# Attention decode with a gated MLP on one core: the order of PE's work behind the turned projection

## The chip, the core and the metric

One core of a Trainium2 chip runs the whole program in one launch. The metric is device time in microseconds; the median of the shown runs counts. Engines: PE (TensorE, matmuls), DVE (VectorE), ACT (ScalarE), POOL (GpSimd), SP (SyncE, which issues the transfers).

## The reference, cut to what matters

```
x = A_x                                    # 4 x 1 x 512
sa, ca, ga, sb, cb, gb = split(silu(c) @ w_mod)
h = layernorm(x) * (1 + ca) + sa
x = x + ga * attention(h)                  # A: 32 heads, 4096 cached keys, 128 per head, 4 batch rows
h = layernorm(x) * (1 + cb) + sb
x = x + gb * mlp(h)                        # B: gelu(h @ w_in), halves z1 and z2,
                                           #    z1 * (w_sp * layernorm(z2) + b_sp) @ w_out
# attention: q = h @ wq; p = softmax(q . k / sqrt(128)); (p @ v) @ wo
```

One query per batch row meets 4096 cached keys and values in each of 32 heads, all in bf16: 268 MB of cache are read once. The MLP is small (512 to 1792, and 896 to 512).

## The kernel before, in words

The cache is worked through in tiles of four heads (NT = 32 of them, numbered by i). The first 30 come in pairs, eight heads of one batch row; the last two, N0 = 30 and L = 31, hold the last eight heads of the last batch row (BL = 3), four each, and are not paired. For each tile DVE multiplies keys by the query (mult, L384) and sums over the head's width together with PE (reduce_d, L392; sum8, L415; sum_rest, L404), DVE finds the maximum, and ACT makes the exponentials (exps, L458), which it writes to pbd. Then PE forms the products with the value tile.

These products come in two forms. pv and pv_some (L513) take four positions of the cache at once: the stationary operand is a slice of pbd (16 columns for an unpaired tile), 512 columns of values stream through, and four such matmuls are placed side by side in the array, at columns 0, 32, 64 and 96. What they leave in PSUM (the tile ops, one of two) holds wanted blocks and others. o_pick takes the wanted ones out on DVE (one L522 and three L526, into osb), and o_cols (L538) adds up and turns them into columns with a matmul; o_scale (L561) divides by the softmax sum and writes to oTp. The second form, o_last with part 2, 3 or 4 (L549), takes a position at a time with the values stationary and gives columns at once, in the PSUM tile qps. For the last tile L, parts 0 and 1 (32 of 128 positions each) go the first way, and parts 2, 3 and 4 (32, 16 and 16) the second; o_first (L555) adds the picked result of parts 0 and 1 to the same sum in qps. The parts follow the five pieces in which the last value tile is loaded (TAIL, load, L142).

The projection with wo: for all heads but the last four, a head's columns have to be dealt out first to fit the layout in which wo was loaded (deal, L640, PE; dealt, L652 and L658, DVE; then o_proj4, L617). The last four heads need none (o_proj, L607). For three head groups the projection makes rows (project, L670); turn (L682, L617 and L607) turns these and adds the heads of the other three batch rows: the turned projection. x1 and the statistics of its layer norm follow for all batch rows (normed: L234, L219, L224, L240, L243, L219, L224, L228, L229). The last batch row lacks its last eight heads there. They are added as `last` afterwards (L801 to L804), and this row gets statistics of its own (L805, a third L219). Then come the MLP (gates L852, L877), the gate weights (L885) and the output (L922, L923).

normed sends two matmuls to PE with DVE work between them, and takes two hooks, which the call before does not use: `then` runs after the first matmul is put in the queue, `last` before the second.

The order of the work is written out by hand: each engine runs its instructions in the order in which the code calls them, and waits only where data or a buffer is not ready. All transfers of this part are issued from SP in order: value tile N0 (4 MB into buffer C), the five pieces of value tile L (into buffer B), two halves of w_in, w_out, two pieces of the MLP's last weights. Eight semaphores go around among the transfers, so that an issue waits for the landing of the eighth transfer before it: w_out's for value tile N0, the next one's for the first piece of tile L, the output's for the third piece.

Of the kernel before, what the change touches and what calls it, by code (L numbers as in the profile page):

```python
# [49 lines left out]
def kernel(  # L50
# [25 lines left out]
    NJ = SK * HQ // P  # L76
    NP = 2 * NJ
    R = P // HQ
    G = 4
    NT = B * H // HQ  # L80
    GP = H // HP - 1
    N0 = NT - 2
# [6 lines left out]
    L = NT - 1  # L89
# [18 lines left out]
    def ps_sm(shape, dtype=F32):  # L108
        return psum.tile(shape, dtype, name="sm", bufs=3)
# [98 lines left out]
    def bc(ap, n):  # L208
        return ap[:, None, :].to_broadcast([P, n, ap.shape[-1]])
# [7 lines left out]
    def across(rhs, mat):  # L217
        ps = ps_sm(list(rhs.shape))
        nc.tensor.matmul(ps, lhsT=mat, rhs=rhs, start=True, stop=True)  # L219
        return ps  # L220

    def summed(pool, ps, name):
        r = pool.tile([P, ps.shape[1]], F32, name=name)
        nc.vector.tensor_reduce(out=r, in_=ps, axis=AX.X, op=ALU.add)  # L224
        return r

    def rsqrt(dst, src, scale, bias=0.0):
        nc.scalar.activation(out=dst, in_=src, func=AF.Ln, bias=bias, scale=scale)  # L228
        nc.scalar.activation(out=dst, in_=dst, func=AF.Exp, scale=-0.5)  # L229

    def normed(pool, src, name, then=None, last=None):

        sb = pool.tile([P, B, DJ], F32, name=f"sb_{name}")
        nc.vector.tensor_copy(out=sb, in_=src.rearrange("p j b -> p b j"))  # L234
        m = across(sb, inv_d)
        if then:
            then()
        m = summed(pool, m, f"m_{name}")
        xc = pool.tile([P, DJ, B], F32, name=f"xc_{name}")
        nc.vector.tensor_tensor(out=xc, in0=src, in1=bc(m, DJ), op=ALU.subtract)  # L240
        sq = pool.tile([P, B, DJ], F32, name=f"sq_{name}")
        xb = xc.rearrange("p j b -> p b j")
        nc.vector.tensor_tensor(out=sq, in0=xb, in1=xb, op=ALU.mult)  # L243
        if last:
            last()
        v = summed(pool, across(sq, inv_d), f"v_{name}")
        rs = pool.tile([P, B], F32, name=f"rs_{name}")
        rsqrt(rs, v, 1.0, eps)
        return xc, rs
# [125 lines left out]
    def pair(i):  # L375
        return i < N0
# [124 lines left out]
    def ops_of(i):  # L501
        return opss[i // 2 % 2 if pair(i) else i % 2]

    def pv(i):
        n = (NP if pair(i) else NJ) // G
        pv_some(i, 0, n, n)

    def pv_some(i, m0, m1, end):
        pb, vt, rows = (pbd8, bufC, G * HP) if pair(i) else (pbds[:, i % 4], vts[i], G * HQ)
        for m in range(m0, m1):  # L510
            n = slice(m * G, (m + 1) * G)
            g = R * (m % 4)
            nc.tensor.matmul(  # L513
                ops_of(i)[g:g + rows], lhsT=pb[:, n, :], rhs=vt[:, n, :],
                start=(m < 4), stop=(m >= end - 4), tile_position=(0, g),
            )

    def o_pick(i):
        ops = ops_of(i)
        sel = sels[HP if pair(i) else HQ]  # L520
        osb = wk.tile([P, DH], F32, name="osb", bufs=2)
        nc.vector.tensor_scalar(  # L522
            out=osb, in0=ops[:, 0, :], scalar1=sel[:, 0:1], scalar2=None, op0=ALU.mult
        )
        for g in range(1, G):
            nc.vector.scalar_tensor_tensor(  # L526
                out=osb, in0=ops[:, g, :], scalar=sel[:, g:g + 1], in1=osb,
                op0=ALU.mult, op1=ALU.add,
            )
        st[i, "osb"] = osb  # L530

    def o_cols(i):
        if pair(i):
            op = ps_sm([P, P])
            nc.tensor.transpose(op, st.pop((i, "osb")), ident_f)
        else:
            op = ps_sm([P, HQ])
            nc.tensor.matmul(op, lhsT=st.pop((i, "osb")), rhs=sel4, start=True, stop=True)  # L538
        st[i, "op"] = op

    def o_last(i, part):
        n0, n1 = sum(TAIL[:part]), sum(TAIL[:part + 1])
        if part < 2:
            pv_some(i, n0 // G, n1 // G, sum(TAIL[:2]) // G)
            return
        if part == 2:
            st[i, "op"] = psum.tile([P, HQ], F32, name="qps", bufs=1)
        for k in range(n0, n1):
            nc.tensor.matmul(  # L549
                st[i, "op"], lhsT=vts[i][:, k, :], rhs=pbds[:, i % 4, k, :],  # L550
                start=(part == 2 and k == n0), stop=(k == NJ - 1),
            )

    def o_first(i):
        nc.tensor.matmul(st[i, "op"], lhsT=st.pop((i, "osb")), rhs=sel4, start=False, stop=False)  # L555

    def o_scale(i):
        op = st.pop((i, "op"))
        if not pair(i):
            q0 = (i - N0) * HQ  # L560
            nc.vector.tensor_tensor(  # L561
                out=oTp[:, NT // 2 - 1, q0:q0 + HQ], in0=op, in1=st.pop((i, "rz")), op=ALU.mult
            )
            return
        g, b = divmod(i // 2, B)
        if b == 0:
            st["P", g, "o"] = wk.tile([P, B, HP], F32, name="oU")
        o = st["P", g, "o"]
        nc.vector.tensor_reduce(
            out=o[:, b, :], in_=op.rearrange("p (c q) -> p q c", q=HP), axis=AX.X, op=ALU.add  # L570
        )
        if whole(i):
            nc.vector.tensor_tensor(
                out=oTp[:, g * B:g * B + b + 1], in0=o[:, 0:b + 1],
                in1=st.pop((i, "rz")).rearrange("p (b q) -> p b q", q=HP), op=ALU.mult,
            )
# [7 lines left out]
    tl = Arena(bufC, 32 * KB, 64 * KB)  # L584
# [28 lines left out]
    def o_proj4(wp, j, bs, start):  # L613

        od = st["od", GP, bs.start]
        for r in range(HQ):
            nc.tensor.matmul(  # L617
                wp[:, j, 0:bs.stop - bs.start], lhsT=wo_sb[:, GP * HP + r, j:D:DJ], rhs=od[:, r, :],
                start=start and r == 0, stop=False, skip_group_check=True,
            )  # L620
# [15 lines left out]
    def deal(k, bs=slice(0, B)):  # L636
        n, nb = HP if k < GP else HQ, bs.stop - bs.start
        pp = ps_sm([P, n, nb, n])
        for r in range(n):
            nc.tensor.matmul(  # L640
                pp[:, r], lhsT=picks[n][:, r, :],
                rhs=oTp[:, k * B + bs.start:k * B + bs.stop, 0:n], start=True, stop=True,
            )
        st["pp", k, bs.start] = pp
# [3 lines left out]
    def dealt(k, b0=0):  # L648
        pp = st.pop(("pp", k, b0))
        n, nb = pp.shape[1], pp.shape[2]  # L650
        ow = own if n == HP else own[:, 0:n * nb, 0:n]
        nc.vector.tensor_tensor(  # L652
            out=ow, in0=pp.rearrange("p r b h -> p (r b) h"),
            in1=bc(mask8 if n == HP else mask4, n * nb), op=ALU.mult,
        )
        od = late.tile([P, n, nb], BF16, name=f"od{k}{b0}")
        with nc.allow_low_precision("all but one term of each sum are zero"):
            nc.vector.tensor_reduce(  # L658
                out=od.rearrange("p r b -> p (r b)"), in_=ow, axis=AX.X, op=ALU.add
            )  # L660
        st["od", k, b0] = od
# [115 lines left out]
    nc.vector.tensor_tensor(out=acc, in0=wp, in1=gaT, op=ALU.mult)  # L777
    x1 = x1w[:, :, 0:B]
    nc.vector.tensor_tensor(out=x1, in0=acc, in1=xT, op=ALU.add)
    xc, rs2 = normed(tl, x1, "ln2")  # L780
    pv(N0)
    o_last(L, 0)
    o_pick(N0)
    o_cols(N0)
    o_scale(N0)
    o_last(L, 1)
    deal(GP, slice(BL, B))
    dealt(GP, BL)
    o_pick(L)
    o_last(L, 2)  # L790
    o_first(L)
    wp = ps_sm([P, DJ, 1])
    for j in range(DJ):
        o_proj4(wp, j, slice(BL, B), j == 0)
    o_last(L, 3)
    o_last(L, 4)
    o_scale(L)
    for j in range(DJ):
# [155 lines left out]
```

## Time and profile before

| | |
|---|---|
| runs shown | 665.11, 665.56, 667.5 us; median 665.56 |
| profiled execution | 667.08 us, span 665.04 us, mean granted clock of PE 0.744 |
| busy share of the span | PE 48%, DVE 86%, ACT 26%, POOL 3% |
| read from HBM | 282.73 MB, 425 GB/s over the span |
| L513 on tile N0 (32 matmuls) | from 643.73 us, for 3.59 us |
| L219, two norm matmuls | 641.90 and 643.20 us, 0.61 us each |
| pick on DVE (L522 and three L526) | from 647.38 and from 650.45 us |
| L549, 32 and 32 matmuls | from 649.98 and from 652.98 us |
| last o_scale (L561) | 654.01 us |
| issue of the output (L923) | 662.72 us |

Times inside the execution are microseconds from the start of its span. A line such as L513 is the line of the kernel before. The chain of waits goes back from the last instruction, at each step to what released it. Matmuls overlap in PE's pipeline, so their ends are modelled. The clock that PE was granted is given as a share of the full one.

### The profile page before, as it was taken

What the parts mean: (1) busy time and instruction counts of PE and PEld (TensorE: products, weight loads), DVE (VectorE), ACT (ScalarE), POOL (GpSimd) and SP (SyncE); (2) the same over time, 40 slices, a digit from 0 to 9 for tenths busy, and PEclk for the clock granted to TensorE, in tenths of its full rate; (3) what the DMA queues carried; (4) which work ended last, traced back from release to release, by engine and by line L of the source; (5) the groups of instructions that cost most, each with busy time, mean ns of one, the idle gap of its engine ahead of it and who ended that gap; (6) DMA issues with size and microseconds to landing.
All of it is one profiled execution on the core that took longest, in us unless ns stands there. A gap on an engine that the chain in (4) does not pass through costs nothing.

```text
span 665.0 us, 5225 instructions
## 1 busy us (share of the span) xinstructions
PE 318.1 (48%) x2134; PEld 137.4 (21%) x2134; DVE 571.1 (86%) x403; ACT 171.3 (26%) x284; POOL 20.0 (3%) x57
## 2 busy tenths in 40 slices
PE   1563543646152364625246461434646243465885
PEld 0221111212021121202112120211212021122344
DVE  3259999989898998989899897989989898999823
ACT  1210606032050604205060410506032050605212
POOL 3000000000000000000000000000000000003100
PEclk9988787857677786767778676787867578787865
DMA  8999999999999999999999999999999999999995
GB/s 362 451 431 430 441 435 442 435 442 435 434 410 441 435 430 441 435 438 439 422 434 442 422 427 441 438 438 442 422 434 435 430 434 439 416 437 430 425 411 205
DMA packets 9356, 283.07 MB, mean 426 GB/s; under 512 B 876, under 2 KB 2804, under 8 KB 3956
## 3 DMA queue, kind: packets, MB, share of 16 engines
q1 hardware_dynamic: 9312, 282.73, 98.6%
q8 instruction: 16, 0.26, 0.1%
q14 instruction: 8, 0.07, 0.0%
q10 hardware_dynamic: 20, 0.01, 0.0%
HBM read 282.73 MB, written 0.00 MB: 425 GB/s over the span
## 4 chain that ended last, share of the span: by engine, by line
DMA 60%; DVE 17%; PE 17%; ACT 4%; issue 1%; POOL 0%; SPq 0%; DVEq 0%; ACTq 0%
DMA bC<-in_A_v_cache_dram 44%; DMA bA<-in_A_k_cache_dram 12%; PE ops L513 10%; DVE bA L384 7%; DVE S L404 5%; ACT pbd L458 3%; PE red L392 3%; DMA bC<-in_w_mod_dram 3%; DVE bB L384 1%; DVE S L415 1%; DMA bC<-in_B_b_sp_dram 1%; PE sm L670 1%; PE qps L319 1%; DVE osb L526 1%; PE sm L311 1%
## 5 line engine op out<-in xcount | busy, mean ns | idle before, releaser
L458 ACT ACTIVATE pbd<-S,nb 32x256 bf16<-32x256 f32 x120 | 154.2, 1519 | 424.9 <-DVE nb L445 423.7
L384 DVE TENSOR_TENSOR bA<-bA,qbp 128x8192 bf16<-128x8192 bf16 x32 | 141.1, 4411 | 25.3 <-DMA bA<-in_A_k_cache_dram 25.3
L392 PE MATMUL red<-bB,ident_bf 128*128 128x512 bf16 x344 | 97.2, 442 | 116.4 <-DVE bB L384 116.3
L392 PE MATMUL red<-bA,ident_bf 128*128 128x512 bf16 x332 | 94.0, 443 | 113.6 <-DVE bA L384 113.4
L392 PEld LDWEIGHTS <-ident_bf 128*128 128x128 bf16 x676 | 73.2, 110 | 344.2 <-issue 176.2
L384 DVE TENSOR_TENSOR bB<-bB,qbp 128x8192 bf16<-128x8192 bf16 x28 | 123.7, 4417 | 15.0 <-DMA bB<-in_A_k_cache_dram 15.0
L513 PE MATMUL ops<-bC,pbd 128*32 128x512 bf16 (+1 forms) x992 | 88.4, 534 | 70.3 <-DMA bC<-in_A_v_cache_dram 65.3
L404 DVE TENSOR_REDUCE S<-bA 128x48 f32<-128x6144 bf16 x15 | 98.1, 6541 | 0.0
L404 DVE TENSOR_REDUCE S<-bB 128x48 f32<-128x6144 bf16 x14 | 91.6, 6542 | 0.0
L513 PEld LDWEIGHTS <-pbd 128*32 128x32 bf16 (+1 forms) x1008 | 37.4, 128 | 119.9 <-issue 65.1
L458 ACT ACTIVATION_READ_ACCUMULATOR pbd<-S,nb 32x1 f32 x120 | 58.6, 489 | 0.0
L415 DVE TENSOR_REDUCE S<-red 128x64 f32<-128x512 f32 x64 | 43.7, 683 | 4.3 <-PE red L392 4.3
L472 POOL TENSOR_TENSOR rsb<-maskd,rs 128x8 f32<-128x8 f32 x15 | 3.9, 260 | 581.3 <-ACT pbd L458 581.3
L384 DVE TENSOR_TENSOR bB<-bB,qbo 128x8192 bf16<-128x8192 bf16 x4 | 17.6, 4412 | 0.0
L526 DVE SCALAR_TENSOR_TENSOR osb<-ops,m,osb 128x128 f32<-128x128 f32 x45 | 15.8, 351 | 1.6
L491 PE MATMUL sm<-rsb,inv_d 128*128 128x32 f32 (+2 forms) x12 | 3.1, 356 | 15.2 <-POOL rsb L472 14.4
L458 ACT ACTIVATE pbd<-S,nM 32x128 bf16<-32x128 f32 x8 | 4.6, 576 | 13.7 <-POOL pbd L718 12.5
L283 DVE SCALAR_TENSOR_TENSOR bC<-sm,bC 128x16 f32<-128x16 f32 x1 | 0.2, 173 | 8.5 <-PE sm L269 8.5
L428 DVE TENSOR_REDUCE mrow<-S 128x1 f32<-128x256 f32 (+1 forms) x17 | 6.9, 404 | 0.6
L631 POOL COPY bA<-ident_bf 128x1024 bf16<-128x1024 bf16 (+1 forms) x2 | 6.5, 3272 | 0.0
L319 PE MATMUL qps<-bC 128*128 128x256 bf16 (+1 forms) x16 | 4.5, 383 | 4.1 <-ACT qbp L329 2.8
L360 DVE COPY modT<-sm 128x48 f32<-128x48 f32 x1 | 0.2, 208 | 7.0 <-PE sm L357 7.0
(160 smaller groups left out, 139.5 us busy)
## 6 DMA issues: line engine op xcount, KB each, us to landing
bA<-in_A_k_cache_dram SPq DMA_DIRECT2D x2, 4096.0 KB, 32.1
bC<-in_A_wq_dram SPq DMA_DIRECT2D x1, 4096.0 KB, 12.2
bB<-in_A_k_cache_dram SPq DMA_DIRECT2D x1, 4096.0 KB, 41.5
bB<-in_A_k_cache_dram SPq DMA_DIRECT2D x2, 2048.0 KB, 40.8
bC<-in_A_v_cache_dram SPq DMA_DIRECT2D x1, 4096.0 KB
bA<-in_A_wo_dram SPq DMA_DIRECT2D x3, 1024.0 KB, 36.8
bB<-in_A_v_cache_dram SPq DMA_DIRECT2D x3, 1024.0 KB, 17.4
bC<-in_w_mod_dram SPq DMA_DIRECT2D x1, 2560.0 KB, 17.9
```

Source lines behind the costliest of these rows:

```text
L311: nc.tensor.matmul(qr[R * q:R * (q + 1)], lhsT=hT[:, k, :], rhs=wq_v[:, k, gs, q, :], start=(k == 0), stop=(k == DJ - 1), tile_position=(0 ...
L319: nc.tensor.matmul(qp[:, 0:npair], lhsT=eb2[k][:, b].rearrange("p k q r -> p (k q r)"), rhs=qrow[:, h, k:2 * npair:2], start=(k == 0), sto ...
L384: nc.vector.tensor_tensor(out=kt, in0=kt, in1=bc(q, KC), op=ALU.mult)
L392: nc.tensor.matmul(red, lhsT=ident_bf, rhs=kt[:, :, m * rd:(m + 1) * rd], start=(m == 0), stop=(m == DH // rd - 1),)
L404: nc.vector.tensor_reduce(out=st[i, "S"][:, n0:NJ], in_=kts[i][:, n0:NJ, :], axis=AX.X, op=ALU.add)
L415: nc.vector.tensor_reduce(out=st[i, "S"][:, kc * KC:kc * KC + on_pe(i, kc)], in_=st.pop((i, "red", kc)), axis=AX.X, op=ALU.add,)
L428: nc.vector.tensor_reduce(out=mrow, in_=S, axis=AX.X, op=ALU.max)
L458: nc.scalar.activation(out=pbd8[r, :, 2 * q + h] if pair(i) else pbds[r, i % 4, :, q], in_=S[r, :], func=AF.Exp, bias=nM[r, h:h + 1], scal ...
L513: nc.tensor.matmul(ops_of(i)[g:g + rows], lhsT=pb[:, n, :], rhs=vt[:, n, :], start=(m < 4), stop=(m >= end - 4), tile_position=(0, g),)
L526: nc.vector.scalar_tensor_tensor(out=osb, in0=ops[:, g, :], scalar=sel[:, g:g + 1], in1=osb, op0=ALU.mult, op1=ALU.add,)
L631: nc.gpsimd.tensor_copy(out=picks[n].rearrange("p r (a u) -> p r a u", a=n), in_=ident_bf.rearrange("p (u r) -> p r u", r=n)[:, :, None, : ...
L670: nc.tensor.matmul(wp, lhsT=od[:, r, :], rhs=wo_sb[:, k * HP + r, :], start=(k == 0 and r == 0), stop=(k == GP - 1 and r == HP - 1),)
```

## The change

Only the calls behind the turned projection are put in another order; no operation is added or removed. The 32 products of tile N0 are divided into 8, 16 and 8: eight ahead of normed, sixteen in its hook `then` (after the first norm matmul), eight in its hook `last` (before the second). Part 1 of the last tile moves ahead of o_pick(N0), so that it stands right behind part 0. Part 2 stands ahead of o_pick(L). The projection of the last row's dealt heads (o_proj4) and part 3 now stand ahead of o_first, which adds the picked half.

```
-    xc, rs2 = normed(tl, x1, "ln2")
-    pv(N0)
+    nv = NJ // G
+    pv_some(N0, 0, nv // 4, nv)
+    xc, rs2 = normed(
+        tl, x1, "ln2",
+        lambda: pv_some(N0, nv // 4, 3 * nv // 4, nv), lambda: pv_some(N0, 3 * nv // 4, nv, nv),
+    )
     o_last(L, 0)
     o_pick(N0)
+    o_last(L, 1)
     o_cols(N0)
     o_scale(N0)
-    o_last(L, 1)
     deal(GP, slice(BL, B))
     dealt(GP, BL)
+    o_last(L, 2)
     o_pick(L)
-    o_last(L, 2)
-    o_first(L)
     wp = ps_sm([P, DJ, 1])
     for j in range(DJ):
         o_proj4(wp, j, slice(BL, B), j == 0)
     o_last(L, 3)
+    o_first(L)
     o_last(L, 4)
     o_scale(L)
```

By engine: the order on DVE, ACT, POOL and SP is the same as before. On PE the eight products now stand behind the last L607 of the turned projection and ahead of the first L219, the other 24 between the two L219, part 1 ahead of L538, and L555 behind L617 and the first 16 of the second L549 group. Lines of the changed kernel from L786 on are numbered higher, by four from o_last(L, 4) on.

## Prediction

> **What bounds the kernel now.** I read the page first, for the share of the transfers, then the chain of waits in the last 25 us, then the DMA queue and the granted clock there.
>
> ```profile
> span 665.0 us, 5225 instructions
> DMA 60%; DVE 17%; PE 17%; ACT 4%; issue 1%; POOL 0%; SPq 0%; DVEq 0%; ACTq 0%
> ```
>
> For 640 us the caches stream in at 425 GB/s, and nothing of the change touches that. What can move is the end, after the last row's products become possible. The chain of waits there (start, length, engine, tile, line):
>
> ```profile
> 641.90 0.62 PE sm L219 x2
> ...
> 643.20 0.61 PE sm L219 x2
> 643.80 3.55 PE ops L513 x30
> ...
> 647.38 0.36 DVE osb L522
> ...
> 649.03 0.35 PE sm L538 x2
> 649.39 0.54 PE ops L513 x8
> ...
> 650.53 0.27 DVE osb L522
> ...
> 652.00 0.59 PE qps L555 x2
> 652.59 0.52 PE sm L617 x16
> 653.12 0.87 PE qps L549 x32
> 653.98 0.02 issue
> 654.01 0.17 DVE oTp L561
> ```
>
> See in it that the 32 products of tile N0 (L513, value tile in bC) start only after both norm matmuls (L219), and that the chain goes on through two picks on DVE (L522 and three L526, 1.51 us each). After the second pick come three pieces of PE work in a row: o_first (L555), the dealt heads (L617), parts 3 and 4 of the last row (L549). Two of these don't need the pick.
>
> Could the products start earlier? Their value tile must have landed. In the SP queue the issue of w_out waited 9.4 us for that transfer and went at 640.69:
>
> ```profile
> 640.69 0.38 SPq L600 DMA_DIRECT2D bA<-in_B_w_out_dram  x1
> 643.13 6.59 SPq L602 DMA_DIRECT2D bA<-in_w_mod_dram  x1
> ```
>
> So it is there by 640.69, 0.4 us before the turned projection ends on PE (last L607 641.14). The next issue waits for part 0 of the last tile: 643.1. By the issue-to-landing times part 3 is there at 649.3 (627.10 + 22.2). My estimates by the rate between these two (2.5 MB in 6.2 us): part 1 645.6, part 2 648.1, part 4 650.5. The halves of w_in land at 652.6 and 654.8 (629.59 + 23.0, 630.95 + 23.8), so w_out, as large as a half, at about 657.0; most of the gate weights at 658.2 (643.13 + 15.1), their small rest about 658.5.
>
> The clock, from the table of stretches (length, PE busy and instructions, clock, DMA share, GB/s):
>
> ```profile
> 637.98:641.40 3.42, 3.16 (x39) 0.50 0.88 374
> 641.40:644.81 3.41, 2.22 (x16) 0.50 1.01 425
> 644.81:648.22 3.41, 3.37 (x32) 0.50 1.00 410
> 648.22:651.64 3.42, 1.89 (x46) 1.00 1.03 423
> ```
>
> The products of N0 run at half clock; full clock comes when they are over.
>
> **The change, part by part.** No instruction is added or taken away; PE's order changes, and on DVE, ACT, POOL and SP the order stays. Row prices: the 32 products start at 643.73 and part 0 behind them at 647.11, so a group of four side by side takes 3.38 / 8 = 0.42 us at half clock, and the last ends 0.25 later. A matmul behind them starts about 0.07 before that end (L640 at 649.86, the products before it end 649.93).
>
> 1. *Eight products ahead of the norm.* They start 0.06 before the last L607 ends, at 641.08, and end at 641.08 + 2 x 0.42 + 0.25 = 642.18. DVE's three steps to the norm's input (L777, L779, L234, until 641.84) lie beside them. The first L219 was ready at 641.90 and now starts at 642.11: 0.21 late, ends 642.72.
> 2. *Sixteen and eight more between the statistics.* From 642.65, 6 x 0.42 + 0.25: end 645.44. DVE's three steps after the first statistic (0.60 us) are hidden. The second L219 was ready at 643.34 but now queues until 645.37 and ends 645.98; before it ended at 643.81. Who waits? DVE's L224 (646.00 to 646.17), two ACT and two POOL instructions, needed by the gates at 655 at the earliest: covered by 8 us. But L224 stands ahead of the pick on DVE, so the pick starts at 646.21, not at 645.46.
> 3. *First pick.* 646.21 instead of 647.38: 1.17 earlier, end 647.72. Meanwhile PE does parts 0 and 1 of the last row (645.91 + 4 x 0.42 + 0.25 = 647.85); both are landed.
> 4. *o_cols (L538).* Starts 647.86. It took 0.35 in the stretch at full clock; the like L555 took 0.59 at half clock, and I take that: 0.24 lost, end 648.45.
> 5. *deal.* Before, part 1's products (0.54) stood between L538 and L640, and L640 started 0.27 after the end of L561; without them about 0.04 after it: 0.23 won. L640 at 648.70, second pick 0.59 later (650.45 - 649.86) at 649.29, end 650.79 instead of 651.95: 1.16 earlier.
> 6. *Part 2, dealt heads, part 3 ahead of o_first.* PE from 648.88: 0.94 + 0.52 + half of 0.87 = 650.78, just under the pick's end at 650.79. So o_first runs from 650.83 to 651.42. Behind it only part 4 is left: 0.44 instead of 0.52 + 0.87. The 0.52 of L617 and 0.44 of part 3 leave the path.
> 7. *End.* L561 is due at 651.9 instead of 654.01. Sum: 1.17 - 0.24 + 0.23 + 0.52 + 0.44 = **2.1 us**. The rest runs as before if its weights are there: gates at 655.3 (second half of w_in 654.8), L877 at 657.6 (w_out 657.0), L885 at 658.4 (658.2; its last four, near 658.8, need the 658.5). All just fit, and no more than 0.5 us is left.
>
> Contention: two POOL steps (L810, L811, 0.21 each) now fall beside the first pick; L812 on POOL ran beside L803 and L804 on DVE, which took 0.16 and 0.17 like L801 without it, so nothing is charged.
>
> Not seen before is a norm matmul inside the products. Bounds for the two new breaks in them: nothing (that wins back the 0.18 of run-out charged at each, 0.36) up to another 0.25 each (a second run-out, -0.5). I stay at one run-out, as between part 1 and L640. [...]
>
> The profiled execution's own time is 667.08 for a span of 665.04; by the sum it would be 665.0 and 662.9. The shown runs have a median of 665.56 (665.11 to 667.5), so the profiled one is 1.5 above; taken from the median: 663.5.
>
> **The rivals.**
> - *Full clock early.* The clock changes on a grid of 3.41 us. From 641.40 to 644.81 PE would hold 0.5 + 2.2 us of products and 0.6 of L219. A stretch at half clock with 2.17 us busy (566.30 to 569.72) was not followed by full clock, one with 3.41 (569.72 to 573.13) was; the turned projection with 3.16 us of tiny matmuls was not. If this one counts, from 644.81 a group takes 0.22 (64 products in 3.57), L219 and L538 0.35: first pick at 645.73, second ends 650.1, part 4 starts at its landing 650.5, L561 at 651.0. That is 3.0, but L877 would then stand at 656.75 and wait for w_out, until about 657.1: 2.6 us, **663.0**. [...]
> - *Transfers end it.* If w_out and the gate weights land about 1.2 us later against PE than estimated, L877 waits until 658.2: gain 1.5, **664.1**. For it: the DMA share is 1.0 until 655. Against: every step above fits.
> - *Late value tile: slower.* PE takes its work in order, so the first L219 now queues behind products that wait for N0's value tile. If that lands d after 641.08, everything in the new order moves by d; in the old one both L219 lie beside the wait, and only d beyond 2.65 (643.73) costs. From d = 2.1 the change loses, at 2.65 and more 0.55: **666.1**. Against: it landed 0.4 before. The landing can slip, but 2.5 us is more than the spread of all shown runs, 2.4.
>
> **How the numbers follow.** Forecast 0.55, early clock 0.22, transfers 0.13, late tile 0.06, something unseen 0.04. Range: down to the early clock less the 0.45 between the shown median and the fastest run (662.5), up to the forecast plus the 1.9 up to the slowest run (665.4), which holds the transfers too: 662.4 to 665.5. Half a per cent, about what a measurement here can tell from no change, is 3.3 us: under 662.2 lies only the early clock with a lucky median, 0.08; above 668.9 only the unseen, 0.03; between 0.89.
>
> **What would show it.** Right: L513 on bC from about 641.1 with L219 in two gaps, first pick near 646.2, second pick's end near 650.8, 16 L549 behind L555, L561 near 651.9, output issue near 660.6. Wrong: PE waiting for a transfer at L513, L549 or L877; full clock from 644.8; more than 0.25 us between the products and L219; the second pick ending before part 3, so that PE and not DVE leads.

## The result, and the profile after

| | before | after |
|---|---|---|
| median of 22 runs | 667.09 us (665.02 to 667.78) | 664.34 us (664.04 to 665.91) |
| ratio after / before | | 0.9969, 95% interval 0.9961 to 0.9977 |
| span of the profiled execution | 665.04 us | 662.33 us |
| output issued (L923, now L927) | 662.72 us | 659.89 us |

The ratio makes 2.1 us of gain (0.31%). The 22 runs of before fall in two groups with nothing between: seven from 665.02 to 665.97 and fifteen from 666.84 to 667.78. The three shown at first had two of the lower group among them. After has one group, with 19 of 22 runs between 664.04 and 664.85. In the profiled pair the span is 2.7 us shorter and the output is issued 2.8 earlier, since before was profiled in a run of the upper group (667.08).

The chain of waits in the last 25 us of after (start, length, what) has no engine left in it up to the matmuls with w_out:

```profile
625.08 15.46 DMA bC<-in_A_v_cache_dram
640.54 0.02 issue
640.55 16.52 DMA bA<-in_B_w_out_dram
657.07 0.05 issue
657.11 0.92 PE qps L881 x28
```

Before, this stretch was a row of PE and DVE steps. Now the chain runs from the landing of value tile N0 (640.54) to that of w_out (657.07), which L881 (L877 before) waits for. Such a chain names only what ended last at each step, not by how much. The timeline of after (start, length, engine, line, operation; behind it idle time and who ended it):

```profile
640.86 1.03 PE L513 MATMUL ops<-bC,pbd 128*16 128x512 bf16 x8
641.83 0.61 PE L219 MATMUL sm<-bC,inv_d 128*128 128x16 f32 x2
642.37 2.55 PE L513 MATMUL ops<-bC,pbd 128*16 128x512 bf16 x24
644.84 0.39 PE L219 MATMUL sm<-bC,inv_d 128*128 128x16 f32 x2
645.37 0.34 DVE L522 TENSOR_SCALAR osb<-ops,selg 128x128 f32<-128x128 f32 x1
647.01 0.35 PE L538 MATMUL sm<-m,osb 128*128 128x4 f32 x2 [0.80 <-DVE osb L526]
648.19 0.34 DVE L522 TENSOR_SCALAR osb<-ops,selg 128x128 f32<-128x128 f32 x1
649.77 0.57 PE L555 MATMUL qps<-m,osb 128*128 128x4 f32 x2
650.42 0.50 PEld L549 LDWEIGHTS <-bB 128*128 128x128 bf16 x16 [0.18 <-DMA bB<-in_A_v_cache_dram]
651.05 0.16 DVE L561 TENSOR_TENSOR oTp<-qps,rz 128x4 bf16<-128x4 f32 x1 [1.36 <-PE qps L549]
657.11 0.82 PEld L881 LDWEIGHTS <-bA 128*128 128x128 bf16 x28 [0.41 <-DMA bA<-in_B_w_out_dram]
```

The products stand around the two norm matmuls as the diff has it; the two picks and L561 are 2.0, 2.3 and 3.0 us earlier than before; and weight loads wait for transfers where none did: 0.18 us for part 4, 0.41 for w_out, and 0.17 and 0.20 for part 2 and the gate weights. The table of stretches of after, by PE alone (length, PE busy and instructions, clock, DMA share, GB/s):

```profile
641.19:644.60 3.41, 3.41 (x34) 0.50 1.01 424
644.60:648.01 3.41, 2.27 (x35) 1.00 1.00 411
648.01:651.42 3.41, 3.06 (x87) 0.50 1.03 426
```

So in this execution the clock was full from 644.60 to 648.01; before, it was full from 648.22 to 651.64.

### The profile page after: what moved, and what is told of

Read it like the earlier page. It is cut to its first block, busy times and chain, and to the rows that moved or that the text cites. A ratio compares the mean times of both kernels' runs of the same rounds, so it can differ in the third digit from the quotient of the medians.

```text
span 662.3 us, 5225 instructions
## 1 busy us (share of the span) xinstructions
PE 317.5 (48%) x2134; PEld 136.7 (21%) x2134; DVE 570.8 (86%) x403; ACT 171.3 (26%) x284; POOL 20.0 (3%) x57
## 4 chain that ended last, share of the span: by engine, by line
DMA 61%; DVE 21%; PE 12%; ACT 4%; issue 1%; POOL 0%; SPq 0%; ACTq 0%; DVEq 0%
DMA bC<-in_A_v_cache_dram 42%; DMA bA<-in_A_k_cache_dram 12%; PE ops L513 8%; DVE S L404 7%; DVE bA L384 7%; DVE bB L384 3%; ACT pbd L458 3%; DMA bC<-in_w_mod_dram 3%; DMA bA<-in_B_w_out_dram 2%; PE red L392 2%; DVE S L415 2%; DMA bC<-in_B_b_sp_dram 1%; PE qps L319 1%; PE sm L311 1%; ACT qbp L329 0%
```

## The experiments

Times are medians. A ratio is to the kernel before, run on the same chip in the same set: its median was 666.96 for e1, e2, e3 and e6, and 666.41 for e5, e7, e8 and e12. The changed kernel itself was not run in these two sets; where it is compared, the ratios are given too.

**One half of the change at a time.** *e1_products_only*, the division of N0's products alone:

```
-    xc, rs2 = normed(tl, x1, "ln2")
-    pv(N0)
+    pv_some(N0, 0, nv // 4, nv)
+    xc, rs2 = normed(tl, x1, "ln2", <products 8 to 24>, <products 24 to 32>)
     o_last(L, 0)                                  # from here as before
```

> Only the products of tile N0 are divided around the norm statistics; the rest stands as before. Theory T (the divided products keep PE busy enough that the clock is full from about 644.6, and in the whole change the landing of w_out is what ends it): the first pick starts near 645.4 instead of 647.4, L538 takes 0.35, and since the end is then still later than the landing of w_out, the whole 2.0 us stay: 2.0 us less than before. Rival P (the forecast's own path at half clock, no transfer in it): pick 1.2 earlier, L538 at 0.59: 0.9 to 1.0 less than before.

Measured: 665.42 us, ratio 0.9971 (0.9959 to 0.9982), 1.9 us less (1.5 by the medians); the profiled span is 1.6 shorter. Its trace:

```profile
645.83 0.34 DVE L522 TENSOR_SCALAR osb<-ops,selg 128x128 f32<-128x128 f32 x1
652.45 0.16 DVE L561 TENSOR_TENSOR oTp<-qps,rz 128x4 bf16<-128x4 f32 x1 [2.06 <-PE qps L549]
```

Neither theory stands as written. The norm matmuls took 0.61 each, as P has it, and part 0's eight products, until 646.66, took 1.03, as at half clock; the first pick is 1.55 earlier than before, between P's 1.2 and T's 2.0; and L538 took 0.36, as T has it. *e2_heads_only*, the rest of the change alone:

```
     xc, rs2 = normed(tl, x1, "ln2")               # as before
     pv(N0)
     o_last(L, 0)
     o_pick(N0)
+    o_last(L, 1)                                  # from here as in the change
```

> Only the later part: part 1 ahead of the pick's columns, part 2, dealt heads and part 3 ahead of the picked half's matmul; the products of N0 stand undivided behind the norm as before. Both theories: the clock is as before, 0.23 + 0.52 + 0.44 = 1.2 us less than before. What tells them apart is the sum: by T, 2.0 (products alone) and 1.2 (this) make 3.2, more than the change gives (2.1 to 2.7), since w_out's landing takes the rest; by P, 0.9 and 1.2 make the 2.1 of the change, with nothing taken.

Measured: 665.80 us, ratio 0.9978 (0.9965 to 0.9992), 1.5 us less, span 1.3 shorter. Its trace:

```profile
650.11 0.34 DVE L522 TENSOR_SCALAR osb<-ops,selg 128x128 f32<-128x128 f32 x1
652.72 0.16 DVE L561 TENSOR_TENSOR oTp<-qps,rz 128x4 bf16<-128x4 f32 x1 [1.11 <-PE qps L549]
```

L561 is 1.29 earlier than before. Of this 0.10 is an earlier start (L538 at 648.93 instead of 649.03); the rest is the 1.19 of its terms (0.23 + 0.52 + 0.44). Both halves pay by themselves. Whether their sum is more than the whole these runs don't settle: 3.4 by the ratios, but with intervals of 0.8 and 0.9 to each side, and 2.9 against 2.7 by the spans.

**The last weights.** *e3_no_last_weights*: the changed kernel without the transfers of w_out and of the gate weights.

```
-        nc.sync.dma_start(out=wout_sb, ...)
-        for ks in KG:
-            nc.sync.dma_start(out=wg_sb[:, ks], ...)
```

> The changed kernel without the transfers of w_out and of the gate weights (both matmul groups read values of w_in in their place, so that part of the computation is left out). T: L877's wait for w_out (0.24 on PE, 0.41 on its weight loads) and L885's for the gate weights go, the end comes 0.3 to 0.5 us earlier than in the changed kernel, 2.5 to 3.2 less than before. P: nothing waits for them, the same time as the changed kernel within 0.1.

Measured: 664.38 us (ratio 0.9968) against 664.34 (0.9969) of the changed kernel. T expected 0.3 to 0.5 less and was wrong: the waits for w_out cost nothing that can be measured. From the first gate matmul to the output's issue it is 5.34 us here, 5.45 in after and 5.33 before, so 0.1. With w_out gone, the chain of waits in e3 runs through the landing of part 4 of the last value tile, at 650.49. *e5_gate_first*: the same two transfers, in the other order.

```
-        nc.sync.dma_start(out=wout_sb, ...)
         for ks in KG:
             nc.sync.dma_start(out=wg_sb[:, ks], ...)
+        nc.sync.dma_start(out=wout_sb, ...)
```

> The changed kernel with the gate weights' two transfers ahead of w_out's: w_out lands about 1.2 us later (658.3 instead of 657.1), the gate weights 2.2 earlier. By the run without these transfers their wait costs 0.1 us in the changed kernel, so L877 is just at the edge and each us later costs a us: 1.0 to 1.2 more than the changed kernel, less about 0.2 for the gate weights' matmuls, which then stand ready behind: 0.8 to 1.2 more. If the slack were as large as the forecast's 0.6 us: 0.4 to 0.6 more.

Measured: 665.52 us (all eleven runs between 665.29 and 665.85), 1.2 more than the changed kernel (1.3 by the ratios, 0.9988 and 0.9969). Its timeline:

```profile
658.59 0.83 PEld L881 LDWEIGHTS <-bA 128*128 128x128 bf16 x28 [1.74 <-DMA bA<-in_B_w_out_dram]
```

w_out came 1.5 us later, and 1.2 of that were paid in the medians, all of it in the trace (output issued at 661.37 instead of 659.89). So in the changed kernel w_out is just at the edge: it costs nothing now, and nearly every microsecond that it came later would cost one.

**The clock in the products.** *e6_filler*: the kernel before with eight useless matmuls where the change puts products.

```
+    filler(2)                                     # 512 columns each
-    xc, rs2 = normed(tl, x1, "ln2")
+    xc, rs2 = normed(tl, x1, "ln2", lambda: filler(4), lambda: filler(2))
     pv(N0)
```

> The kernel before, with eight added matmuls of 512 columns (identity times a row of wo, result not used) in the places that the products take in the change: two ahead of the first norm matmul, six between the two; the products of N0 still follow undivided. It adds 3.4 us of PE work at half clock. T (this activity frees the clock near 644.6): the 32 products run at 0.22 us a group instead of 0.42, from 645.2 to about 647.2, so the pick starts at about the same time as before: between 0.3 less and 0.3 more. P (clock stays at half): the products start 1.4 to 1.6 later and the time is 1.4 to 1.6 us more than before.

Measured: 665.97 us, ratio 0.9984 (0.9970 to 0.9998): with more work it is not slower, but about 1 us faster, with an interval that nearly reaches none. T's time (0.3 less to 0.3 more) is at the edge of this interval, P's (1.4 to 1.6 more) far outside. Two views of it, timeline and stretches:

```profile
643.50 0.45 PE L219 MATMUL sm<-bC,inv_d 128*128 128x16 f32 x2
643.88 2.03 PE L513 MATMUL ops<-bC,pbd 128*16 128x512 bf16 x32
```

```profile
640.78:644.19 3.41, 3.41 (x14) 0.50 1.01 428
644.19:647.60 3.41, 2.15 (x40) 1.00 1.01 414
```

The 32 products took 2.03 us instead of 3.59. So here a stretch filled with streamed columns, with norm matmuls among them, was followed by full clock. How much of the gain in time comes from that this trace can't say: its turned projection was over 1.4 us earlier than before, for the reason of the next part. In the changed kernel the early clock is worth little. In e3's trace the clock was half until 647.06, the first pick began at 645.59 instead of 645.37, and part 4 at 650.53 instead of 650.43; the output was issued at 659.87, as in after. In e5's trace both norm matmuls took 0.61, too. L561 came at 651.16 in e3 and 651.21 in e5, 0.1 to 0.2 later than the 651.05 of after.

**What splits the runs of before.** In the traces of e1, e3 and e6 the turned projection was over 1.4 to 1.8 us earlier than before (first DVE step behind it, L777, in e3 L774, at 639.77, 639.41 and 639.82 instead of 641.18). Such traces are called early here, and that of before late. The difference came from one reduction for the last tile, 20 us ahead (timeline of before, then of e1):

```profile
618.33 4.88 PE L392 MATMUL red<-bB,ident_bf 128*128 128x512 bf16 x16
```

```profile
618.19 3.61 PE L392 MATMUL red<-bB,ident_bf 128*128 128x512 bf16 x16
```

The reduction ends 1.41 us earlier in e1, and from its end to L777 it is 17.97 us in both: all of the lead is kept. The traces of after and e2 are late ones, too (reduction 4.87 and 4.91 us, L777 at 640.97 and 641.07). The stretches show why it is 4.88 or 3.61. Before, PE's idle time from 615.3 to 617.7 lay nearly whole in one stretch, and the next was at half clock (before, then e1):

```profile
614.09:617.50 3.41, 1.21 (x6) 1.00 0.85 368
617.50:620.92 3.42, 3.26 (x17) 0.50 0.86 364
```

```profile
612.59:616.01 3.42, 2.80 (x13) 1.00 1.19 517
616.01:619.42 3.41, 1.67 (x16) 1.00 0.72 310
619.42:622.83 3.41, 3.41 (x40) 1.00 0.91 384
```

In the trace of before the clock changes from 597 us on at 597.03, 607.27, 617.51, 620.92, 637.99, 648.23 and 651.64, always whole multiples of 3.41 us apart. In e1 this grid of stretches stood 1.5 us otherwise, the idle time was shared by two stretches, and the clock stayed full. The other traces with this idle time (2.36 us in each) fit. In the six late ones (before, after, e2 and the three unchanged runs below) one stretch holds nearly all of it, with 1.05 to 1.23 us of busy PE, and the next is at half clock. In the four early ones (e1, e3, e5, e6) a border of the grid falls inside it, at 616.00 to 616.89; no stretch has less than 1.67 busy, and the clock stays full. How much idle time is too much is not shown by this: after's stretch with 2.27 busy (644.60 to 648.01) was followed by half clock, too. *e7_before_kept_full* and *e8_after_kept_full* fill 1.9 us of that idle time, in the old and in the new order:

```
         reduce_d(i, 1)
+        if i == L - 1:
+            for m in range(8):                    # 512 columns each, result not used
+                nc.tensor.matmul(fill, lhsT=ident_bf, rhs=kts[i][:, KC:NJ, 0:RD], ...)
```

> The kernel before with eight added matmuls of 512 columns (result not used) in PE's idle time of 1.8 us ahead of the last rows' statistics near 615.3, which fill that clock stretch. Theory S (the phase of the clock grid decides whether PE drops to half clock for the reduction at 618 us, which then takes 4.9 instead of 3.6 us and brings the project and the turned projection 1.2 to 1.3 us later; that is what splits the runs of the kernel before into those near 665.3 and those near 667.2): nearly all runs near 665.3, mean 1.2 to 1.7 less than before, span near 663.2. Rival Q (the split has another cause, transfers for one): spread as before, and no gain, or up to 0.4 more for the added work.

Measured: 665.65 us, all eleven runs between 664.71 and 666.08, where the kernel before went from 665.03 to 668.60; ratio 0.9989 (0.9980 to 0.9998), 0.9 less by the means. The reduction took 3.61 us and the late runs are gone, as S said, but the gain is smaller than its 1.2 to 1.7: in this trace the 32 products took 3.59, as at half clock, and behind them L538 took 0.56 and part 1 1.03 (0.35 and 0.61 before); the second pick came 3.71 after the first instead of 3.07.

> The changed kernel with the same eight matmuls. S: the turned projection ends near 639.8 in every run, but the products of N0 wait for their value tile's landing near 640.65, and part 4 for its own near 650.4, so nothing is won: the same as the changed kernel within 0.3 (664.1 to 664.5). Q (in the new order too the path is PE's and DVE's): it would go down with the earlier projection, 1.0 to 1.2 less than the changed kernel (663.2).

Measured: 664.38 us, ratio 0.9973, as the changed kernel. Its timeline has the reason:

```profile
640.84 1.03 PE L513 MATMUL ops<-bC,pbd 128*16 128x512 bf16 x8 [1.28 <-DMA bC<-in_A_v_cache_dram]
```

PE was ready 1.28 us earlier, and waited for value tile N0. *e12_no_wo_last* is e8 with 0.5 MB less ahead of that tile:

```
-        nc.sync.dma_start(out=wo_last, ...)
```

> As e8_after_kept_full, and the 0.5 MB transfer of the last four heads' rows of wo is left out (those matmuls read another part of wo, so that part of the computation is left out); every later transfer can land 1.24 us earlier. S with the new order bound by the value tiles' landings: products start at 639.85 to 639.9 instead of 640.7, part 4's landing 1.2 earlier, the time 0.7 to 1.2 less than e8_after_kept_full. Q (bound by engines): the same as e8_after_kept_full.

Measured: 663.63 us, 0.75 less than e8 (1.05 by the means). The products started without a wait:

```profile
639.51 1.03 PE L513 MATMUL ops<-bC,pbd 128*16 128x512 bf16 x8
```

So the changed kernel goes down with the landings, and not with PE's earlier readiness.

**Three more traces of the kernel before** (*b1_look*, *b2_look*, *b3_look*), to see the other kind of run in it:

> The kernel before, unchanged, one look. Theory S: a run with its own time near 665.3 shows the reduction at 618 us in 3.6 us and the turned projection over at 639.8; one near 667 shows it in 4.9 us and over at 641.0. Rival Q: no such tie.

> The kernel before, unchanged, a second look, to see the other kind of run. By S and Q as for the first look.

> The kernel before, unchanged, a third look, to see the other kind of run. By S and Q as for the first look.

All three were late: own times 668.72, 667.60 and 667.60, the reduction 5.17, 5.28 and 5.23 us, L777 at 641.76, 641.98 and 641.70. They agree with S: here the reduction began 0.02 to 0.22 us behind the border of the stretch at half clock, in the trace before 0.82 behind it. But an unchanged run near 665.3 wasn't caught in a trace; that its reduction takes 3.61 is inferred from e7 and from e1 and e6, which are unchanged up to there. Nor are there always two groups: in the two sets of the experiments the runs of before, from 665.00 to 668.88, fill the gap. A reduction between 3.61 and 5.28, by where the grid stands, fits that, but it makes 1.7 us in these traces, and the rest of the spread isn't explained.

## Why the prediction was right, point by point

The forecast was 2.1 us less; measured were 2.1 by the ratio. The forecast time, 663.5, is 0.8 below the measured 664.34. It was taken from the median of three runs; with 22 that median is 1.5 higher, and 2.1 less would have been 665.0, 0.7 too high, as the medians themselves are 2.75 apart. The agreement in size is in part luck, as it has two errors in it that cancel. Against the mean of after, the upper group of before, with the profiled run, is 2.8 slower; the lower group is 1.0 slower. The bounds of the range, worked out as 662.5 and 665.4, were put down as 662.4 and 665.5; nothing hangs on that.

1. *Eight products ahead.* Right: 640.86, end 641.89, the first L219 0.06 before that end. One run-out per break, as charged (0.06 less), and no further price for a full-size matmul between tiled ones was measured: from the first product to L219 it took 0.97 us.
2. *The other 24 and the first pick.* Forecast 646.21, came 645.37. Of these 0.84 us, 0.28 are an earlier start and shorter gap, 0.25 products that ran at full clock after 644.60, 0.22 a faster L219 (0.39 instead of 0.61), 0.09 the way over L224.
3. *L538 at 0.59*: wrong. It took 0.35 here and 0.36 in e1 and e3, at full clock each time, in the stretch behind the products. In e7, where part 1 behind it took 1.03, as at half clock, it took 0.56. With point 2 that is the rival *full clock early*, which I gave 0.22; of its figures (first pick 645.73, part 4 at its landing 650.5, L881 near 657.1, 2.6 us) the trace has 645.37, 650.43, 657.11 and 2.7.
4. *Deal without products ahead of it, heads and part 3 off the path*: right. L538's end to the second pick 0.83 (forecast 0.84); L555 directly behind the pick; behind it only part 4. e2 measured these terms alone: 1.19, without its earlier start.
5. *Transfers just fit*: right for the forecast's own times, and the edge is where it was put: with the path a further 0.8 earlier, part 4 and w_out were waited for. e5 shows what lies beyond.
6. *The failed step* is one that I took as fixed: the turned projection ends at 641.14, and the value tile is there 0.4 us before. That holds in the late runs alone. In the early traces of the new order (e1, e3, e5, e8) PE is ready before the tile and waits 1.17 to 1.32 us for it, until 640.69 to 640.93. The first norm matmul, which the old order lets run at once (640.19 in e7), queues behind these products (641.80 in e8). That is the mechanism of my slower rival at d = 1.2 to 1.3, below its point of 2.1: it takes part of the gain, not all. By its arithmetic 2.1 - 1.2 = 0.9 us is left; e7 and e8, the two orders in early runs, differ by 1.1 in their means.

## What to carry to other kernels

Before adding up the steps behind a matmul chain, look at several executions: the profiled one can lie at one end of their spread, and the gain of a reordering can differ from one end to the other (here 1.0 and 2.8 us). Work put into an engine's idle time ahead of a chain pays up to the landing of its data; from there on the transfers are what is left to tune, as e12 and e5 show in both directions. When one order has taken the waits out of the engines, a transfer that lands just in time can become a bound, though no profile of the old order shows it.

## What the runs showed of the hardware

- 2.4 us of idle time on PE cost 1.3 to 1.7 us or nothing, by where it fell on the clock's grid: the reduction behind it took 4.87 to 5.28 us in six traces and 3.61 in four. The loss was still there 20 us later, at the end of the turned projection.
- Eight useless matmuls of 512 columns didn't make a kernel slower (665.97 against 666.96, ratio 0.9970 to 0.9998): in the trace the 32 products behind them took 2.03 instead of 3.59 us.
- PE's busy time in a stretch doesn't tell whether the next gets full clock. After's stretch from 637.77 to 641.19, filled for the most part with matmuls of three or four columns, had 3.42 us busy and was followed by half clock; before's from 644.81 to 648.22, with 512-column products, had 3.37 and was followed by full clock.
- The turned projection's matmuls of four columns didn't care for the clock: before, the first two of L682 took 0.63 us together at full clock (637.42), the three pairs behind them 0.62 each at half clock (from 638.33). The whole took 3.72 us from its first L682 to its last L607 before (637.42 to 641.14) and in e1 (636.01 to 639.73). L538, of four columns too, took 0.35 at full clock in after and 0.56 in e7.
